# Both score halves of a head pair in one TensorE group, over two double banks of PSUM

## The chip, the core and the metric

The kernel runs on one core of a Trainium2 chip. The metric is the device time of one execution in microseconds. The core has a matrix engine (TensorE, PE in the profile; its weight loads are PEld), a vector engine (VectorE, DVE), an activation engine (ScalarE, ACT), GpSimd (POOL, which issues most loads here) and SyncE (SP, which issues the stores and the DMA transposes). Each takes its own instructions in the order written; semaphores hold them together. TensorE writes to PSUM, which has eight banks of 128 partitions x 512 fp32.

## The reference

Sparse causal attention over 8 batches, 8 heads, 576 positions and head size 64, and then an MLP with an ELU on its output rows.

```python
scores = scale * np.matmul(q, k.transpose(0, 1, 3, 2))
mask_local = (rel >= 0) & (rel < 32)                       # heads 0 to 3
mask_strided = (rel >= 0) & (pos[None, :] % 32 == pos[:, None] % 32)   # heads 4 to 7
attn = softmax of the masked scores
x = (attn @ v) as [4608, 512]
h = x @ w_in                                               # [512, 2048]
g = np.where(h > 0.0, h, np.exp(np.minimum(h, 0.0)) - 1.0)
out = g @ w_out                                            # [2048, 512], fp32
```

## The kernel before

The 4608 rows of x are cut into nine chunks of 512. The main loop runs over nb = 0 to 9; its iteration nb has 16 steps s, and each step issues, in this order: the attention pieces of gap 2s, `moe_in(nb, s)`, the pieces of gap 2s + 1, `moe_out(nb - 1, s)`. `moe_in` makes one [128 x 512] block of h: four products (L532) into a bank of the ring `hps`, the exponential on ACT (L553), a clamp on DVE (L560) and a maximum on DVE that also reads the bank (L562). `moe_out` adds four of the sixteen products of an output block (L572) in a bank of the ring `ops`; every fourth one is followed by the copy to SBUF on ACT (L576) and the store on SP. The schedule is manual: each engine's order is the order in which the program issues.

The attention of batch nb + 1 lies in the gaps of iteration nb. A batch has four pairs of heads: s0 and s1 (strided), l0 and l1 (local). Pair i takes its gaps from `start + pitch * i` on, by the offsets in `TIMES`: t_q and t_k (transposes of q and k on TensorE; left out for strided pairs from batch `BY_DMA` = 3 on and for local ones from batch `EARLY` = 4 on, where DMA transposes do it), two halves u = 0 and 1 of the scores, two halves of AV, x_out, and v_in. `scores(u)` makes four or six products of 64 rows each (L422) into a double bank, takes the exponential on ACT (L430) and multiplies with the mask on DVE (L437). `av(u)` multiplies the probabilities with v and a column of ones (L454) into one bank of `ring`, and DVE takes the reciprocal of the sums (L462) and scales (L463) into x. `x_out` transposes x on TensorE into a bank of `ring` (L490 strided, L503 local) and copies it to xT (ACT at L497 and L499 for strided pairs, DVE at L507 for local ones); from batch 4 on the pair l0 does this by a DMA transpose (L482). `halo` copies rows of v on DVE (L411), in the pair s1, two gaps ahead of its second AV. For batches 3 to 7 the list ends with

```python
(at[6] + (b > 1 and pr.strided), pr.x_out), (at[5] - 2, pr.halo)
```

so a strided pair's x_out comes one gap later than a local one's.

A `Ring` gives out its banks: one that was not used yet, or else the one used longest ago. `share` sets the four rings `sc` (scores), `hps`, `ops` and `ring` for each iteration. From the second iteration on `sc` has one double bank, `pair_a`; a second one, `pair_b`, serves the opening and is then split into the two banks `b_halves` for `hps`. `ops` has one bank, singles[3], wherever attention of batch 2 or later runs beside it.

Of the kernel before, what the change touches and what calls it, by code (L numbers as in the profile page):

```python
# [10 lines left out]
F32 = mybir.dt.float32  # L11
# [5 lines left out]
PSUM = bass.MemoryType.PSUM  # L17
# [13 lines left out]


PIECES = (-2, -1, 0, 2, 3, 5, 7, 0)
TIMES = (
    None,
    (4, 6, (-3, -2, 0, 2, 4, 6, 9, 3)),
    (6, 6, (-3, -2, 0, 2, 4, 6, 8, 0)),
    (2, 7, PIECES),
)


# [15 lines left out]
def kernel(  # L57
# [23 lines left out]
    inner = ctx.enter_context(ExitStack())  # L81
# [5 lines left out]

    ps = inner.enter_context(tc.tile_pool(name="ps", bufs=1, space=PSUM))
    pair_a = ps.tile([128, 2, 512], F32, tag="pair_a")
    singles = [ps.tile([128, 512], F32, tag=f"single{i}", name=f"single{i}")  # L90
               for i in range(4)]

    used = []

    class Ring:
        def __init__(self, *banks):
            self.banks = banks

        def next(self):

            for bank in self.banks:
                if all(bank is not u for u in used):
                    break
            else:
                bank = next(u for u in used if any(u is b for b in self.banks))
                used[:] = [u for u in used if u is not bank]
            used.append(bank)
            return bank


    rings = {}

    def share(sc, hps, ops, ring):
        rings.update(sc=Ring(*sc), hps=Ring(*hps), ops=Ring(*ops), ring=Ring(*ring))
# [2 lines left out]
    opening = ctx.enter_context(ExitStack())  # L117
    p_p0 = opening.enter_context(tc.tile_pool(name="probs0", bufs=8))
    p_k = opening.enter_context(tc.tile_pool(name="keys", bufs=1))
    ps_open = ctx.enter_context(ExitStack())  # L120
    ps_b = ps_open.enter_context(tc.tile_pool(name="ps_b", bufs=1, space=PSUM))
    pair_b = ps_b.tile([128, 2, 512], F32, tag="pair_b")

    def bf16_bank():
        return rings["ring"].next().bitcast(BF16)
# [32 lines left out]
    BY_DMA = 3  # L158
# [46 lines left out]
    def transpose_batch(b):  # L205

        if b >= BY_DMA:
            for name, to in (("q", qT), ("k", kT)):
                nc.sync.dma_start_transpose(out=to["str"][b % 2],
                                            in_=nat[name, "str"][b % 3])  # L210
        if b >= EARLY:
            for name, to, o in (("q", qT, 0), ("k", kT, 32)):
                for a in range(2):
                    nc.sync.dma_start_transpose(
                        out=to["loc"][b % 2][:, a, o:o + 640].rearrange(
                            "p (i r) -> p i r", r=128),
                        in_=nat[name, "loc"][b % 3][:, 640 * a:640 * a + 640])

    def load_batch(b):
        for name in "qkv":  # L220
            load_strided(b, name)
        for name in "qkv":
            load_local(b, name)
# [97 lines left out]
    class Pair:  # L321
# [89 lines left out]
                nc.vector.tensor_copy(t[0:32, :, 1:6, 0:D], t[96:128, :, 0:5, 0:D])  # L411

        def scores(self, u):
            sc = rings["sc"].next()
            blocks = self.blocks(u)
            for p, blk, bank, i, nk, nq in blocks:
                at, half = self.place(p, blk)
                d = slice(64 * half, 64 * half + 64)
                kind = "str" if self.strided else "loc"
                c = 0 if self.strided else LB * blk  # L420

                nc.tensor.matmul(sc[:, bank, i * nq:(i + 1) * nq],  # L422
                                 lhsT=kT[kind][self.b % 2][d, at, c:c + 128],
                                 rhs=qT[kind][self.b % 2][d, at, c:c + nq],
                                 start=True, stop=True)
            nk, nq = blocks[0][4:]
            w = len(blocks) // 2 * nq
            pr = (p_p if self.b else p_p0).tile([128, 648], BF16, tag="pr", name="pr")
            halves = pr[0:nk, 0:2 * w].rearrange("k (a x) -> k a x", a=2)
            nc.scalar.activation(halves, sc[0:nk, :, 0:w], ACT.Exp, scale=scale)  # L430
            if not self.strided:
                m = mask_l[:, 288 * u:288 * (u + 1)]
            elif u == 0:
                m = mask_s[0:126, 0:252]
            else:
                m = mask_s3[0:108, 0:324]
            nc.vector.tensor_tensor(halves, halves,  # L437
                                    m.unsqueeze(1).to_broadcast([nk, 2, w]),
                                    op=ALU.mult)
            self.pr[u] = pr  # L440
# [68 lines left out]
    def attention(b, start, pitch, at):  # L509


        gaps = {}
        pairs = [Pair(b, s, hp) for s in (True, False) for hp in range(2)]
        for i, pr in enumerate(pairs):
            for off, piece in ((at[0], pr.t_q), (at[1], pr.t_k),
                               (at[7], lambda pr=pr: pr.v_in(0)),
                               (at[7] + (b > 1), lambda pr=pr: pr.v_in(1)),
                               (at[2], lambda pr=pr: pr.scores(0)),
                               (at[3], lambda pr=pr: pr.scores(1)),
                               (at[4], lambda pr=pr: pr.av(0)),  # L520
                               (at[5], lambda pr=pr: pr.av(1)),
                               (at[6] + (b > 1 and pr.strided), pr.x_out), (at[5] - 2, pr.halo)):
                gaps.setdefault(start + pitch * i + off, []).append(piece)
        return gaps

# [10 lines left out]
    def moe_ahead(c, start, stop):  # L536

        for m in range(AHEAD):
            if start:
                ahead[m] = rings["hps"].next()  # L540
            moe_chunk(0, m, c, ahead[m], start, stop)
# [56 lines left out]
    def range_flag(row_ok16):  # L598
        cnt = rings["ring"].next()
        nc.tensor.matmul(cnt[0:1, 0:1], lhsT=row_ok16, rhs=ones, start=True, stop=True)  # L600
        nc.vector.tensor_scalar(flag, cnt[0:1, 0:1], scalar1=127.5, scalar2=None,
                                op0=ALU.is_le)

    def run(gaps, keys):
        for gap in sorted(g for g in gaps if g in keys):
            for piece in gaps[gap]:
                piece()
# [4 lines left out]
    for step in OPENING:  # L612
        pair, what = step.split(".")
        if pair == "moe":
            if step == parts[0]:

                ps_open.close()
                ps_h = inner.enter_context(tc.tile_pool(name="ps_h", bufs=1, space=PSUM))
                b_halves = [ps_h.tile([128, 512], F32, tag=f"half{i}", name=f"half{i}")
                            for i in range(2)]  # L620
                rings["hps"] = Ring(*b_halves, singles[3])
            moe_ahead(int(what), step == parts[0], step == parts[-1])
        else:
            pairs[pair].step(what)
# [13 lines left out]
    for nb in range(n_chunks + 1):  # L638

        if nb + 1 < B:  # L640
            gaps = attention(nb + 1, *TIMES[min(nb + 1, 3)])
            if nb == 0:
                share([pair_a], b_halves + singles[3:], [], singles[:3])
            elif nb + 1 < EARLY:
                share([pair_a], b_halves, singles[3:], singles[:3])
            else:
                share([pair_a], b_halves + singles[:1], singles[3:], singles[1:3])
        else:
            gaps = {}
            share([], b_halves + singles[:1], singles[2:], singles[1:2])  # L650
        if nb + 3 < B:
            load_batch(nb + 3)
        for s in range(MC):
            if s == 6 and nb > 0 and nb + 2 < B:
                transpose_batch(nb + 2)
            run(gaps, (2 * s,) if s else range(-10, 1))
            if nb < n_chunks:
                moe_in(nb, s)
            run(gaps, (2 * s + 1,))
            if nb == B and s == 4:  # L660
                range_flag(row_ok16)
            if nb > 0:
                moe_out(nb - 1, s)
        run(gaps, range(2 * MC, 1000))
        if nb + 1 == B:
            row_ok16 = range_check()
# [163 lines left out]
```

## Time and profile before

| what | value |
|---|---|
| runs | 334.74, 334.87, 336.98 us; median 334.87 |
| profiled execution | span 333.1 us from its first to its last instruction; the page gives no other time of it |
| TensorE | busy 310.6 us (93%) |
| DVE | busy 246.2 us (74%) |
| ACT | busy 177.8 us (53%) |
| POOL | busy 147.5 us (44%) |
| PE share of the chain that ended last | 81% |
| L572, 128x512 | 145.5 us busy, 379 ns mean |
| L532, 128x512 | 112.2 and 38.8 us busy (two kinds of bank), 383 and 381 ns mean |
| L430, exponential of scores | 39.0 us busy, 650 ns mean |
| L562, DVE maximum | 70.2 and 25.5 us busy, 688 ns mean |
| L576, output copy | 21.1 us busy, 587 ns mean |

A row of the order of time has a start, a duration, an engine, a line, an operation, out<-in by the program's names, the shapes and a count of instructions that follow one another; brackets at its end hold the idle time before it and what ended it. Products are pipelined, so one of them lasts longer than the step from its start to the next one's; the step is what PE's time is made of.

### The profile page before, as it was taken

What the parts mean: (1) busy time and instruction counts of PE and PEld (TensorE: products, weight loads), DVE (VectorE), ACT (ScalarE), POOL (GpSimd) and SP (SyncE); (2) the same over time, 40 slices, a digit from 0 to 9 for tenths busy, and PEclk for the clock granted to TensorE, in tenths of its full rate; (3) what the DMA queues carried; (4) which work ended last, traced back from release to release, by engine and by line L of the source; (5) the groups of instructions that cost most, each with busy time, mean ns of one, the idle gap of its engine ahead of it and who ended that gap; (6) DMA issues with size and microseconds to landing.
All of it is one profiled execution on the core that took longest, in us unless ns stands there. A gap on an engine that the chain in (4) does not pass through costs nothing.

```text
span 333.1 us, 6197 instructions
## 1 busy us (share of the span) xinstructions
PE 310.6 (93%) x2262; PEld 151.8 (46%) x2262; DVE 246.2 (74%) x540; ACT 177.8 (53%) x316; POOL 147.5 (44%) x233
## 2 busy tenths in 40 slices
PE   1886878999999999999999999999999999999993
PEld 0553444555544454444444444444444444444441
DVE  6686689786878778889788878887888666766500
ACT  3747967776446755554555455545554434444310
POOL 8977675998299699969796000000000000000000
PEclk9999979999999999999999999999999999999999
DMA  5999998999999999999999906310001010010111
GB/s 105 147 134 173 168 207 112 128 127 145 158 123 157 141 179 105 125 145 214 118 139 152 131 33 134 89 50 33 31 33 49 31 66 31 31 36 31 64 64 70
DMA packets 100091, 35.09 MB, mean 105 GB/s; under 512 B 77837, under 2 KB 95445, under 8 KB 100053
## 3 DMA queue, kind: packets, MB, share of 16 engines
q0 software_dynamic: 68016, 18.10, 56.4%
q1 hardware_dynamic: 32037, 16.52, 24.3%
q8 instruction: 19, 0.31, 0.5%
q14 instruction: 19, 0.16, 0.2%
HBM read 36.70 MB, written 9.44 MB: 139 GB/s over the span
## 4 chain that ended last, share of the span: by engine, by line
PE 81%; POOL 7%; DVE 4%; DMA 4%; issue 1%; ACT 1%; DVEq 0%; POOLq 0%; ACTq 0%
PE single L572 38%; PE half L532 25%; PE single L532 8%; PE pair_a L422 3%; PE single L454 3%; DMA v_loc<-in_v_dram 2%; DMA w_in_sb<-in_moe_w_in_dram 2%; POOL v_raw L173 1%; POOL v_loc L185 1%; POOL k_str L173 1%; DVE g_sb L562 1%; PE single L490 1%; PE single L366 1%; PE single L503 1%; DVE x_l L463 1%
## 5 line engine op out<-in xcount | busy, mean ns | idle before, releaser
L572 PE MATMUL single<-w_out_sb,g_sb 128*128 128x512 bf16 x576 | 145.5, 379 | 0.0
L532 PE MATMUL half<-xT,w_in_sb 128*128 128x512 bf16 x428 | 112.2, 383 | 0.5 <-DVE xT L507 0.5
L553 ACT ACTIVATE e_sb<-half 128x512 f32<-128x512 f32 x107 | 63.9, 598 | 75.9 <-PE half L532 70.4
L560 DVE TENSOR_SCALAR e_sb<-e_sb 128x512 bf16<-128x512 f32 x139 | 62.2, 447 | 47.1 <-ACT e_sb L553 44.7
L572 PEld LDWEIGHTS <-g_sb 128*128 128x128 bf16 x576 | 52.8, 98 | 59.0 <-issue 1.1
L532 PEld LDWEIGHTS <-w_in_sb 128*128 128x128 bf16 x576 | 51.0, 99 | 53.1 <-issue 1.0
L562 DVE TENSOR_TENSOR g_sb<-e_sb,half 128x512 bf16<-128x512 bf16 x102 | 70.2, 688 | 3.8
L430 ACT ACTIVATE pr<-pair_a 128x576 bf16<-128x576 f32 (+2 forms) x60 | 39.0, 650 | 10.6 <-PE pair_a L422 10.4
L532 PE MATMUL single<-xT,w_in_sb 128*128 128x512 bf16 x148 | 38.8, 381 | 0.0
L553 ACT ACTIVATE e_sb<-single 128x512 f32<-128x512 f32 x37 | 22.1, 598 | 26.8 <-PE single L532 23.6
L576 ACT COPY o_sb<-single 128x512 f32<-128x512 f32 x36 | 21.1, 587 | 20.0 <-PE single L572 19.7
L454 PEld LDWEIGHTS <-pr 128*128 128x128 bf16 (+3 forms) x352 | 21.6, 111 | 16.4 <-issue 3.4
L562 DVE TENSOR_TENSOR g_sb<-e_sb,single 128x512 bf16<-128x512 bf16 x37 | 25.5, 688 | 1.4
L185 POOL DMA_DIRECT2D v_loc<-in_v_dram x32 | 24.0, 779 | 3.2 <-DMA k_loc<-in_k_dram 1.4
L173 POOL DMA_DIRECT2D k_str<-in_k_dram x32 | 20.7, 692 | 5.8 <-DMA w_out_sb<-in_moe_w_out_dram 3.2
L173 POOL DMA_DIRECT2D v_raw<-in_v_dram x32 | 21.0, 718 | 3.1 <-DMA k_str<-in_k_dram 1.9
L173 POOL DMA_DIRECT2D q_str<-in_q_dram x28 | 17.8, 659 | 10.2 <-DMA k_loc<-in_k_dram 6.9
L463 DVE TENSOR_TENSOR x_l<-single,rden 96x384 bf16<-96x384 f32 x32 | 17.7, 553 | 1.1
L437 DVE TENSOR_TENSOR pr<-pr,mask_l 128x576 bf16<-128x576 bf16 x32 | 14.4, 453 | 3.1 <-ACT pr L430 2.9
L463 DVE TENSOR_TENSOR x_s<-single,rden 126x256 bf16<-126x256 f32 (+1 forms) x32 | 15.7, 491 | 1.1
L437 DVE TENSOR_TENSOR pr<-pr,mask_s 126x504 bf16<-126x504 bf16 (+1 forms) x32 | 14.3, 449 | 1.3 <-ACT pr L430 1.1
L454 PE MATMUL single<-v_loc,pr 128*128 128x65 bf16 x192 | 12.3, 204 | 0.9 <-DVE v_loc L411 0.7
(96 smaller groups left out, 246.1 us busy)
## 6 DMA issues: line engine op xcount, KB each, us to landing
out_dram<-o_sb SPq DMA_DIRECT2D x36, 256.0 KB, 2.4
v_loc<-in_v_dram POOLq DMA_DIRECT2D x32, 72.0 KB, 6.8
k_str<-in_k_dram POOLq DMA_DIRECT2D x32, 67.5 KB, 4.3
v_raw<-in_v_dram POOLq DMA_DIRECT2D x32, 67.5 KB, 5.0
w_in_sb<-in_moe_w_in_dram POOLq DMA_DIRECT2D x4, 512.0 KB, 7.7
w_out_sb<-in_moe_w_out_dram POOLq DMA_DIRECT2D x4, 512.0 KB, 12.9
q_str<-in_q_dram POOLq DMA_DIRECT2D x28, 67.5 KB, 5.2
q_loc<-in_q_dram POOLq DMA_DIRECT2D x4, 288.0 KB, 6.4
```

Source lines behind the costliest of these rows:

```text
L173: engine.dma_start(out=t[0:108, h].rearrange("p g d -> p (g d)"), in_=rows[h, :, 0:30, :].rearrange("t (r g) d -> t r (g d)", g=5))
L185: nc.gpsimd.dma_start(out=v_loc[b % 3][32:128, h, :, :D], in_=v[b, h].rearrange("(i p) d -> p i d", p=LB))
L430: nc.scalar.activation(halves, sc[0:nk, :, 0:w], ACT.Exp, scale=scale)
L437: nc.vector.tensor_tensor(halves, halves, m.unsqueeze(1).to_broadcast([nk, 2, w]), op=ALU.mult)
L454: nc.tensor.matmul(av[0:m, p, blk - b0, :], lhsT=self.pr[u][0:nk, o:o + m], rhs=vt[0:nk, 2 * self.hp + p, blk, :], start=True, stop=True)
L463: nc.vector.tensor_tensor(self.x[0:nq, b0:b0 + n].rearrange("q g p d -> q p g d"), av[0:nq, :, 0:n, 0:D], r.unsqueeze(3).to_broadcast([nq, ...
L532: nc.tensor.matmul(hps, lhsT=w_in_sb[:, c, m * 128:(m + 1) * 128], rhs=xT[:, c, nb * N_TILE:(nb + 1) * N_TILE], start=start, stop=stop)
L553: nc.scalar.activation(e_sb, hps, ACT.Exp)
L560: nc.vector.tensor_scalar(e1_sb, e_sb, scalar1=1.0, scalar2=1.0, op0=ALU.min, op1=ALU.subtract)
L562: nc.vector.tensor_tensor(g_of[nb][:, m, :], e1_sb, hps, op=ALU.max)
L572: nc.tensor.matmul(ops, lhsT=g_of[nb][:, m, kk * 128:(kk + 1) * 128], rhs=w_out_sb[:, m, :], start=(m == 0), stop=(m == MC - 1))
L576: nc.scalar.copy(o_sb, ops)
```

## The change

For batches 3 to 7 the offsets `PIECES` = (-2, -1, 0, 2, 3, 5, 7, 0) give way to `WHOLE`: both score halves at 0, AV at 3 and 4, x_out at 6 for every pair. The half u = 0 always goes to `pair_a`, u = 1 always to `pair_b`. `pair_b` is now allocated once, and `b_halves` are views of its two banks. From the iteration with batch 3 on these halves are in the ring for AV and for x_out, and `hps` takes single banks: two with batch 3, as before, and three later, as before. Whenever `pair_b` is given out as a whole, both halves count as just used. The halo moves with the second AV, to offset 2.

```diff
+WHOLE = (-2, -1, 0, 0, 3, 4, 6, 0)
 TIMES = (
...
-    (2, 7, PIECES),
+    (2, 7, WHOLE),
 )
...
+    pair_b = ps.tile([128, 2, 512], F32, tag="pair_b")
+    b_halves = [pair_b[:, i, :] for i in range(2)]
...
-        def next(self):
-
-            for bank in self.banks:
+        def next(self, of=None):
+
+            banks = self.banks if of is None else self.banks[of:of + 1]
+            for bank in banks:
                 if all(bank is not u for u in used):
                     break
             else:
-                bank = next(u for u in used if any(u is b for b in self.banks))
+                bank = next(u for u in used if any(u is b for b in banks))
                 used[:] = [u for u in used if u is not bank]
             used.append(bank)
+            if bank is pair_b:
+                used[:] = [u for u in used if all(u is not h for h in b_halves)]
+                used.extend(b_halves)
             return bank
...
         def scores(self, u):
-            sc = rings["sc"].next()
+            sc = rings["sc"].next(u if self.b >= BY_DMA else None)
...
-                               (at[6] + (b > 1 and pr.strided), pr.x_out), (at[5] - 2, pr.halo)):
+                               (at[6] + (b == 2 and pr.strided), pr.x_out), (at[5] - 2, pr.halo)):
...
             if nb == 0:
                 share([pair_a], b_halves + singles[3:], [], singles[:3])
+            elif nb + 1 < BY_DMA:
+                share([pair_a], b_halves, singles[3:], singles[:3])
             elif nb + 1 < EARLY:
-                share([pair_a], b_halves, singles[3:], singles[:3])
+                share([pair_a, pair_b], singles[1:3], singles[3:], b_halves + singles[:1])
             else:
-                share([pair_a], b_halves + singles[:1], singles[3:], singles[1:3])
+                share([pair_a, pair_b], singles[:3], singles[3:], b_halves)
         else:
             gaps = {}
-            share([], b_halves + singles[:1], singles[2:], singles[1:2])
+            share([], singles[:3], [singles[3], b_halves[0]], b_halves[1:])
```

More of the change, by code (lines that the diff above doesn't have):

```diff
@@ L119 @@
     p_k = opening.enter_context(tc.tile_pool(name="keys", bufs=1))
-    ps_open = ctx.enter_context(ExitStack())
-    ps_b = ps_open.enter_context(tc.tile_pool(name="ps_b", bufs=1, space=PSUM))
-    pair_b = ps_b.tile([128, 2, 512], F32, tag="pair_b")
     def bf16_bank():
@@ L615 @@
             if step == parts[0]:
[L617 to L620, printed above, removed]
                 rings["hps"] = Ring(*b_halves, singles[3])
```

## The prediction

> **What bounds the kernel now.** I read the page, then PE's waits, then the order of time in the five iterations whose attention is that of batches 3 to 7.
>
> ```profile
> span 333.1 us, 6197 instructions
> PE   1886878999999999999999999999999999999993
> PE half L532 <- DVE xT L507: 0.5, 1, 0.5
> ```
> The span is 333.1 us, and the median of the runs is 334.87, so 1.8 us lie around the span; I add differences to the median. The third line is the whole list of PE's waits from 88 us to 275 us: one wait of 0.5 us. In these stages TensorE runs back to back, and only what lengthens or shortens its own queue counts. DVE is the next engine: busy 27.13 of the 32.64 us from 226.59 to 259.23. The work between the products is therefore free as long as it is in time, and late as soon as its due time moves forward.
>
> The price of a group on PE is the step from its first start to the next group's:
>
> ```profile
> 160.28 1.03 PE L532 MATMUL half<-xT,w_in_sb 128*128 128x512 bf16 x4
> 161.14 1.03 PE L572 MATMUL single<-w_out_sb,g_sb 128*128 128x512 bf16 x4
> 162.10 0.28 PE L422 MATMUL pair_a<-qT_str,kT_str 64*128 64x126 bf16 x4
> 162.31 1.04 PE L532 MATMUL half<-xT,w_in_sb 128*128 128x512 bf16 x4
> 163.19 1.03 PE L572 MATMUL single<-w_out_sb,g_sb 128*128 128x512 bf16 x4
> 164.15 0.32 PE L422 MATMUL pair_a<-qT_str,kT_str 64*128 64x108 bf16 x6
> 164.40 1.04 PE L532 MATMUL single<-xT,w_in_sb 128*128 128x512 bf16 x4
> ```
> Four full products take 0.86 us (160.28 to 161.14), 0.216 each. Ahead of scores the step is 0.96: entry into the 64-row form costs **0.10**. The four scores start within 0.065 us, in two couples (a couple runs side by side on the two halves of the rows), and the last couple needs 126/512 of 0.216 = 0.05; yet the next product starts 0.145 after it. So leaving costs **0.09**.
>
> **Gain: two groups become one.** Four pairs in each of five batches lose one entry and one exit: 20 x 0.19 = **3.8 us**. The ten or twelve products themselves remain, and no other work covers this; it comes straight off PE. Bounds: 2.0 if only the entry is saved, 4.2 if the slower first product after the scores (0.226 for 0.216) goes too.
>
> The Trainium skill (TensorEngine Tiling (Array Packing), Key Properties) says that changing the tiling mode, and not just the tile, drains TensorE. A full drain would be the product's 379 ns less its 216 ns step, an estimate of 0.16 us for each switch; 40 switches would then give 6.5 us in place of 3.8, and the sum below would end at 338.6. The trace shows smaller switches, so I keep 3.8.
>
> **Cost: x_out comes sooner than DVE.** Between the second AV product (L454) and the pair's transposes (L490, L503) DVE must do the reciprocal (L462) and the multiplication (L463). Before, a strided pair has three gaps for it (offsets 5 to 8), a local one two (5 to 7). After, all have two (4 to 6), and AV changes parity. An AV in an even gap stands before moe_in, so DVE takes its work ahead of that step's activation; one in an odd gap stands behind moe_in, and its DVE work queues behind the whole chain L553, L560, L562:
>
> ```profile
> 181.02 1.03 PE L532 MATMUL half<-xT,w_in_sb 128*128 128x512 bf16 x4
> 181.89 0.36 PE L454 MATMUL single<-v_loc,pr 128*128 128x65 bf16 x6
> 182.09 0.60 ACT L553 ACTIVATE e_sb<-half 128x512 f32<-128x512 f32 x1 [1.33 <-PE half L532]
> 182.72 0.43 DVE L560 TENSOR_SCALAR e_sb<-e_sb 128x512 bf16<-128x512 f32 x1
> 183.18 0.69 DVE L562 TENSOR_TENSOR g_sb<-e_sb,half 128x512 bf16<-128x512 bf16 x1
> 183.78 0.18 DVE L462 RECIPROCAL rden<-single 96x6 f32<-96x6 f32 x1
> 184.00 0.55 DVE L463 TENSOR_TENSOR x_l<-single,rden 96x384 bf16<-96x384 f32 x1
> ```
> From AV to normalised x it is 184.55 - 181.89 = 2.66 us in an odd gap; ACT had stood idle 1.33, so it is a chain and no backlog. In an even gap (189.01 to 190.81) it is 1.80. Due time after two gaps: AV 0.20 + two groups 1.73 + the transposes of the first half (0.10 strided, 0.13 local), which need only the first AV: 2.04 to 2.06. That a transpose runs up to the second half and then waits shows at 158.13: six transposes took 0.58 in place of 0.42, x being ready at 158.35; a release takes 0.06.
>
> Pair by pair, for batches 4 to 7 (starts 2, 9, 16, 23):
> - s0: AV in gaps 5 and 6, x_out in 8. The second AV is even, but its 0.7 us of DVE work now stand right behind the first AV's, which end 2.56 after an odd gap. 2.56 + 0.70 - 1.02 (the second AV's later start) = 2.24; + 0.06 - 2.04 = **0.25** (0.19 to 0.30 by how far DVE's records overlap).
> - s1: gaps 12 and 13, x_out 15: odd. 2.68 + 0.06 - 2.04 = 0.70. The halo copy (0.49, now in gap 11) and the first normalisation stand ahead and push this step's L560 back by about 0.2; I take **0.80** (0.66 to 0.95).
> - l0: x_out is a DMA from SP's queue; PE waits for nothing. It is issued earlier, behind nothing new.
> - l1: gaps 26 and 27, x_out 29: odd. 2.66 + 0.06 - 2.06 = **0.66** (0.60 to 0.75).
>
> **Cost: two exponentials ahead of an output copy.** There is one bank for L572 (singles[3]), freed by the copy L576 of every fourth moe_out, and in gap 23 the scores of l1 stand just before such a moe_out:
>
> ```profile
> 183.91 0.30 PE L422 MATMUL pair_a<-qT_loc,kT_loc 64*128 64x96 bf16 x6
> 184.01 0.60 ACT L553 ACTIVATE e_sb<-single 128x512 f32<-128x512 f32 x1 [1.33 <-PE single L532]
> 184.51 0.65 ACT L430 ACTIVATE pr<-pair_a 128x576 bf16<-128x576 f32 x1
> 185.22 0.59 ACT L576 COPY o_sb<-single 128x512 f32<-128x512 f32 x1
> 186.21 1.04 PE L572 MATMUL single<-w_out_sb,g_sb 128*128 128x512 bf16 x4
> ```
> The copy ends at 185.81 and its bank is wanted at 186.21. With both exponentials ahead, counted from the scores: L553 0.10, exponentials 0.60 and 1.15 to 1.25, copy 1.70 to 2.00, its end 2.29 to 2.59, release 2.35 to 2.65. PE wants the bank after scores 0.35 and two groups 1.73, at 2.08, since the second score group no longer lies between. That is 0.27 to 0.57; I take **0.40**. Queued behind the waiting L572 is all of PE.
>
> The Trainium skill (TensorEngine Tiling (Array Packing), PSUM Bottleneck) warns that tiling speeds up TensorE but not the emptying of PSUM. By the trace this bites only here: ACT is busy 17.87 of 32.64 us, so as an engine it does not become the bound.
>
> **Edits at nothing.** The scores' second half needs pair_b, the ring of AV and x_out since the last pair. After s0 the ACT copies of x_out (0.61 + 0.20, behind L576) free it at about the same 0.1 us at which it is wanted, since x_out has itself waited; without that wait it would cost 0.2 instead. Masks come earlier and hide under the three gaps to AV. hps keeps its two or three banks; the last iterations only rename theirs.
>
> **Batch 3** transposes its local q and k on PE: t_q (0.48 with its entry) lies in s1's two gaps and leaves 0.3 of its wait, and t_k now stands behind x_out's copies on ACT, so that l0's scores wait some 0.2 for kT. l0's x_out, on PE here, has t_q of l1 ahead of it and is in time. With s0 0.25, l1 0.66 and the copy 0.40: 1.8 us.
>
> **Sum.** Batches 4 to 7: 0.25 + 0.80 + 0.66 + 0.40 = 2.11 each, 8.4; batch 3 1.8; less 3.8: **+6.4 us, 341.3**. All low ends with the full gain give 4 x 1.72 + 1.2 - 4.2 = +3.9; all high ends with a gain of 2.0 give 4 x 2.57 + 2.4 - 2.0 = +10.7.
>
> **Rivals.**
> - *Faster: DVE is early.* The masks leave DVE before AV instead of between the two AVs; were x ready within 2.04 of the odd AV, x_out would wait nowhere. Where the copy's wait then remains, 5 x 0.4 - 3.8 = -1.8 gives 333.1; where the freer engines hide that too, 331.1. It decides from a latency 0.64 shorter. Against it: ACT's idle 1.33 above; the odd latency is a chain that no mask is part of. Chance 0.08: 0.05 for 331.1, 0.03 for 333.1.
> - *A draw.* Half of each wait, with the whole gain: 0.5 x 10.2 - 3.8 = +1.3, 336.2. Waits are not independent: where PE has waited, DVE and ACT have caught up. For it: s0's wait spares the ring's. Chance 0.13.
> - *The halves of pair_b count as one buffer.* Then the second AV waits for the first's normalisation: 2.6 or 1.8 against 1.02, some 1.6 + 0.8 + 1.6 + 0.8 a batch, 24 us, less part of the x_out waits: about 355. Against it: x's halves were told apart at 158.13. Chance 0.04.
> - The forecast, waits as laid out: 0.75.
>
> **Numbers.** About 1% (3.3 us) can be told from no change. Faster by more 0.05; within 1% 0.16 (the draw, and 333.1); slower by more 0.79 (the forecast and the one buffer). The forecast's own range is 338.8 to 345.6; for 8 in 10 I reach down into the draw: 336.5 to 345.6.
>
> **What would show it.** Right: L422 in 20 groups of ten or twelve with one entry each; in PE's waits L490 on DVE x_s some 5 us, L503 on x_l some 3.3, L572 on ACT's L576 some 2; an iteration of batch 5 near 33.9 us in place of 32.64. Wrong: no PE wait on L463, an AV-to-x latency under 2.0 in gaps 13 and 27, or a step before and after the scores that does not shrink.

## The result and the profile after

The changed kernel takes 374.08 us (median of 4 runs), the one before in the same comparison 334.81: a ratio of 1.120, 95% interval 1.115 to 1.125. The forecast was 341.3 in a range of 336.5 to 345.6. The sign was right, the size was off by a factor of six.

The page of the changed kernel. The busy row of PE has lost its nines from the second fifth on, and comes back to them only at the end.

```profile
span 372.2 us, 6161 instructions
PE   1785877787797989888988898889888999979994
```

Between 88 and 275 us TensorE had one wait of 0.5 us before. Now the list of PE's waits over the whole run (columns: total, times, longest) holds these; lines of the changed file stand four lines lower (L458 is AV, L536 moe_in, L576 moe_out, L566 the maximum, L467 the normalisation):

```profile
PE pair_b L536 <- DVE g_sb L566: 10.4, 15, 1.0
PE pair_b L458 <- DVE x_s L467: 10.3, 8, 1.4
...
PE pair_b L458 <- DVE x_l L467: 8.6, 8, 1.8
...
PE pair_b L576 <- DVE flag L605: 1.8, 1, 1.8
```

All of them write to pair_b, and each waits for DVE. A stretch of the order of time in the pair s1 shows what for:

```profile
196.30 0.32 PE L458 MATMUL pair_b<-v_str,pr 126*128 126x65 bf16 x4
...
197.51 0.61 DVE L415 COPY v_loc<-v_loc 32x1280 bf16<-32x1280 bf16 x1
...
198.04 0.16 DVE L466 RECIPROCAL rden<-pair_b 126x4 f32<-126x4 f32 x1
198.24 0.42 DVE L467 TENSOR_TENSOR x_s<-pair_b,rden 126x256 bf16<-126x256 f32 x1
...
198.71 0.37 PE L458 MATMUL pair_b<-v_str,pr 108*128 108x65 bf16 x6 [1.23 <-DVE x_s L467]
```

The first AV (196.30) writes half 0, the second (198.71) half 1. The second starts 0.05 us after DVE has finished reading half 0. It needs nothing from there: its own bank had been free since the exponential of the scores. In the built program the first product of each of the sixteen second AVs of batches 4 to 7 waits by a semaphore for exactly that multiplication, which reads the other half (8 and 8 waits in the list above), so the wait was put there when the program was made; the chip only obeys it. The same is in `moe_in` of the early iterations, where `hps` is made of the two views and each block waits for the maximum of the block before, and at the very end, where the range flag's bank and one of `ops` are the two halves:

```profile
65.82 0.69 DVE L566 TENSOR_TENSOR g_sb<-e_sb,pair_b 128x512 bf16<-128x512 bf16 x1
...
66.56 1.02 PE L536 MATMUL pair_b<-xT,w_in_sb 128*128 128x512 bf16 x3 [0.84 <-DVE g_sb L566]
...
331.02 0.16 PE L604 MATMUL pair_b<-ones,row_ok 128*1 128x1 bf16 x1
333.01 1.02 PE L576 MATMUL pair_b<-w_out_sb,g_sb 128*128 128x512 bf16 x3 [1.83 <-DVE flag L605]
```

Where the time went, by iteration. An iteration is counted from the first weight load of a chunk's moe_in to the next chunk's (chunk 8: to the first load of the moe_out behind it); all 576 of these loads are in each trace. us:

| iteration (attention of batch) | before | after | difference |
|---|---|---|---|
| to the start of chunk 1 | 55.75 | 56.77 | +1.0 |
| chunk 1 (batch 2) | 36.17 | 47.43 | +11.3 |
| chunk 2 (batch 3) | 35.34 | 40.60 | +5.3 |
| chunk 3 (batch 4) | 32.81 | 37.69 | +4.9 |
| chunks 4, 5, 6 (batches 5 to 7) | 32.64 each | 37.68, 37.57, 37.57 | +14.9 |
| chunk 7 | 27.63 | 27.63 | 0 |
| chunk 8 | 27.83 | 29.71 | +1.9 |

Together that is, but for rounding, the difference of the spans, 39.1 us. Chunk 1 is worst, although its offsets were not changed at all: PE waits 10.1 us there for the maximum. Not all of chunk 2's 5.3 is the change: in this execution the granted clock stood at half from 122.5 to 125.9 us (in the one before at 45.4 to 48.8, ahead of chunk 1), which can be up to 1.7 us of it.

One thing went as planned: the two score groups are one.

```profile
183.57 1.03 PE L576 MATMUL single<-w_out_sb,g_sb 128*128 128x512 bf16 x4
...
184.53 0.28 PE L426 MATMUL pair_a<-qT_str,kT_str 64*128 64x126 bf16 x4
184.65 0.31 PE L426 MATMUL pair_b<-qT_str,kT_str 64*128 64x108 bf16 x6
...
184.89 1.04 PE L536 MATMUL single<-xT,w_in_sb 128*128 128x512 bf16 x4
```

From the product group at 183.57 to the next at 184.89 it takes 1.32; less that group's own 0.864, 0.46 for ten score products. Before it was (0.96 - 0.864) + 0.21 and (0.96 - 0.864) + 0.25 in two groups, together 0.65. The gain is 0.19 per pair, the forecast's figure; the step of the first product behind a scores group is 0.01 longer than of the others (0.226 for 0.216), which also happens once in place of twice; with it, and unrounded, a pair gains 0.21.

### The profile page after: what moved, and what is told of

It is laid out like the page before. It is cut to its first block, busy times and chain, and to the rows that moved or that the text cites. A ratio compares the mean times of both kernels' runs of the same rounds, so it can differ in the third digit from the quotient of the medians.

```text
span 372.2 us, 6161 instructions
## 1 busy us (share of the span) xinstructions
PE 308.9 (83%) x2222; PEld 154.6 (42%) x2262; DVE 245.7 (66%) x540; ACT 174.6 (47%) x316; POOL 146.6 (39%) x233
## 4 chain that ended last, share of the span: by engine, by line
PE 60%; DVE 15%; ACT 10%; issue 5%; POOL 4%; DMA 3%; SPq 1%; ACTq 0%; DVEq 0%; POOLq 0%
PE single L536 22%; PE single L576 19%; ACT e_sb L557 6%; PE pair_b L536 6%; PE pair_b L576 6%; DVE g_sb L566 5%; DVE e_sb L564 4%; DVE x_l L467 2%; DMA q_stage<-in_q_dram 2%; PE pair_b L458 2%; DVE x_s L467 1%; ACT pr L434 1%; DMA v_raw<-in_v_dram 1%; PE pair_a L426 1%; PE pair_b L426 1%
## 5 line engine op out<-in xcount | busy, mean ns | idle before, releaser
L557 ACT ACTIVATE e_sb<-single 128x512 f32<-128x512 f32 x118 | 70.6, 598 | 126.2 <-PE single L536 120.8
L536 PE MATMUL single<-xT,w_in_sb 128*128 128x512 bf16 x459 | 120.1, 380 | 1.7 <-issue 0.8
L576 PE MATMUL single<-w_out_sb,g_sb 128*128 128x512 bf16 x463 | 119.5, 381 | 2.0 <-issue 1.4
L566 DVE TENSOR_TENSOR g_sb<-e_sb,single 128x512 bf16<-128x512 bf16 x117 | 80.5, 688 | 4.4
L536 PEld LDWEIGHTS <-w_in_sb 128*128 128x128 bf16 x576 | 53.2, 98 | 69.4 <-issue 15.0
L576 PEld LDWEIGHTS <-g_sb 128*128 128x128 bf16 x576 | 53.5, 98 | 62.4 <-issue 4.9
L536 PE MATMUL pair_b<-xT,w_in_sb 128*128 128x512 bf16 x96 | 27.0, 383 | 14.3 <-DVE g_sb L566 10.4
L458 PEld LDWEIGHTS <-pr 128*128 128x128 bf16 (+3 forms) x352 | 21.4, 109 | 37.3 <-issue 26.5
L434 ACT ACTIVATE pr<-pair_a 128x576 bf16<-128x576 f32 (+2 forms) x40 | 25.5, 636 | 7.4 <-PE pair_a L426 7.3
L557 ACT ACTIVATE e_sb<-pair_b 128x512 f32<-128x512 f32 x26 | 15.6, 599 | 23.9 <-PE pair_b L536 23.1
L576 PE MATMUL pair_b<-w_out_sb,g_sb 128*128 128x512 bf16 x94 | 23.5, 379 | 2.0 <-DVE flag L605 1.8
L580 ACT COPY o_sb<-single 128x512 f32<-128x512 f32 x30 | 17.7, 590 | 11.3 <-PE single L576 11.3
L434 ACT ACTIVATE pr<-pair_b 128x576 bf16<-128x576 f32 (+2 forms) x24 | 16.3, 677 | 1.3 <-PE pair_b L426 1.3
L566 DVE TENSOR_TENSOR g_sb<-e_sb,pair_b 128x512 bf16<-128x512 bf16 x22 | 15.1, 688 | 0.8
L458 PE MATMUL pair_b<-v_str,pr 108*128 108x65 bf16 (+2 forms) x92 | 6.2, 197 | 10.3 <-DVE x_s L467 10.3
L441 DVE TENSOR_TENSOR pr<-pr,mask_s 126x504 bf16<-126x504 bf16 (+1 forms) x32 | 13.8, 457 | 1.3 <-ACT pr L434 1.2
```

Source lines behind the costliest of these rows:

```text
L441: nc.vector.tensor_tensor(halves, halves, m.unsqueeze(1).to_broadcast([nk, 2, w]), op=ALU.mult)
L458: nc.tensor.matmul(av[0:m, p, blk - b0, :], lhsT=self.pr[u][0:nk, o:o + m], rhs=vt[0:nk, 2 * self.hp + p, blk, :], start=True, stop=True)
L536: nc.tensor.matmul(hps, lhsT=w_in_sb[:, c, m * 128:(m + 1) * 128], rhs=xT[:, c, nb * N_TILE:(nb + 1) * N_TILE], start=start, stop=stop)
L557: nc.scalar.activation(e_sb, hps, ACT.Exp)
L566: nc.vector.tensor_tensor(g_of[nb][:, m, :], e1_sb, hps, op=ALU.max)
L576: nc.tensor.matmul(ops, lhsT=g_of[nb][:, m, kk * 128:(kk + 1) * 128], rhs=w_out_sb[:, m, :], start=(m == 0), stop=(m == MC - 1))
```

## Experiments

Two theories. A: the two views of one PSUM tile are held as one buffer, so every write into one half waits for the readers of the other. B: the new order itself (AV and x_out too early for DVE) costs the time. Totals of one kernel spread by a few us with the clock that was granted (the first experiment ran 344.0 and 343.6 at a mean of 0.987, 341.4 and 339.9 at 0.999), so what matters by less is read from the iterations.

### Two buffers, the whole new schedule

```diff
-    pair_b = ps.tile([128, 2, 512], F32, tag="pair_b")
-    b_halves = [pair_b[:, i, :] for i in range(2)]
...
+                b_halves = [ps_h.tile([128, 512], F32, tag=f"half{i}", name=f"half{i}")
+                            for i in range(2)]
...
-            sc = rings["sc"].next(u if self.b >= BY_DMA else None)
+            two = self.b >= BY_DMA and u == 1
+            if two:
...
+                sc = [b_halves[0], b_halves[1]]
...
-            nc.scalar.activation(halves, sc[0:nk, :, 0:w], ACT.Exp, scale=scale)
+            if two:
+                for a in range(2):
+                    nc.scalar.activation(halves[:, a, :], sc[a][0:nk, 0:w], ACT.Exp,
+                                         scale=scale)
```

> The changed kernel with its whole schedule (both score halves in one group, AV at 3 and 4, x_out at 6), but the two banks are two buffers again: the opening has its own double bank, the main loop two single banks half0 and half1; the second score half goes into these two, with one exponential for each in place of one over both. Theory A (the two views of pair_b are held as one buffer, so that a writer of one half waits for the readers of the other): nearly all of the 39 us comes back, and what stays is the forecast's sum, 338.8 to 345.6 us; the waits of L458's AV for the other half's normalisation are gone, and the x_out waits of 0.2 to 0.9 us appear. Theory B (the schedule itself costs it: AV and x_out come too early for DVE, whatever the buffers): stays above 365 us.

342.5 us, ratio 1.020 (1.011 to 1.028): A. Nothing of the order was touched, and 32 of the 39 us are gone; that the split exponential gives nothing of it back shows in the kernel with the old offsets below. Chunk 1 takes 36.17 again, chunk 8 27.83. PE's waits from 91 to 258 us are now led by the ones that the forecast had laid out (L504 and L517 are the transposes in this file, L477 the normalisation, L590 the output copy):

```profile
PE half L504 <- DVE x_s L477: 3.9, 6, 0.9
PE half L517 <- DVE x_l L477: 2.1, 4, 0.6
...
PE single L586 <- ACT o_sb L590: 0.2, 1, 0.2
```

and in s1 one sees the transposes of the first half, then the wait for the multiplication of the second:

```profile
213.80 0.28 PE L504 MATMUL half<-identity,x_s 126*128 126x126 bf16 x2
...
214.28 0.56 DVE L477 TENSOR_TENSOR x_s<-half,rden 108x384 bf16<-108x384 f32 x1
...
214.90 0.32 PE L504 MATMUL half<-identity,x_s 108*128 108x108 bf16 x3 [0.82 <-DVE x_s L477]
```

The output copy's wait stands where it was expected, in l1. It hardly shows in the list, which counts only the idle time behind a product's end: below, the product group ahead of the waiting one (224.16 to 225.19) ends 0.11 us before 225.30, but the step from its start is 1.143 in place of 0.863. The two exponentials of the second half take 0.72 together, for 0.65 of the one over both banks:

```profile
224.05 0.72 ACT L441 ACTIVATE pr<-half 128x288 bf16<-128x288 f32 x2
...
224.63 0.62 ACT L590 COPY o_sb<-single 128x512 f32<-128x512 f32 x1
...
225.30 1.02 PE L586 MATMUL single<-w_out_sb,g_sb 128*128 128x512 bf16 x4
```

### The old schedule on views

```diff
+    pair_b = ps.tile([128, 2, 512], F32, tag="pair_b")
+    b_halves = [pair_b[:, i, :] for i in range(2)]
...
-                b_halves = [ps_h.tile([128, 512], F32, tag=f"half{i}", name=f"half{i}")
-                            for i in range(2)]
```

> The kernel before with its whole schedule, and only the allocation of the changed one: pair_b stays allocated, and half0 and half1, here banks of hps, are views of it. Theory A: PE waits in moe_in for the maximum (L562) of the block before: some 11 us more in the iteration of chunk 1 and about as much in that of chunk 2 (two banks, both views), 4 to 5 us in each of those of chunks 3 to 6 (two views and one single bank), little at the ends: 360 to 378 us in all. Theory B: as before, 335 us.

398.32 us, ratio 1.188 (1.179 to 1.197). The allocation alone, without any change of order, costs more than the change itself, because here the views serve `hps`, the ring of every moe_in, to the end. Chunk 1 takes 13.8 us more (in this execution with 3.4 us at half the clock, up to 1.7 of it), chunk 2 12.0, chunks 3 to 6 4.6 to 5.4 each, near what A gives; chunks 7 and 8 take 6.4 and 7.2 more and what lies ahead of chunk 1 4.5, which I had left out, so the total is above the 378 that I gave. One line has most of it:

```profile
PE pair_b L531 <- DVE g_sb L561: 53.9, 62, 2.4
```

### Two buffers, the old offsets

```diff
-WHOLE = (-2, -1, 0, 0, 3, 4, 6, 0)
+WHOLE = (-2, -1, 0, 2, 3, 5, 7, 0)
```
(and the extra gap for a strided pair's x_out again)

> As the one with two buffers again, but with the old offsets from the fourth batch on (score halves at 0 and 2, AV at 3 and 5, x_out at 7 or 8): the new places of the banks and the two exponentials for the second half, without merged groups. Theory A: 334 to 336 us, as before: places and exponentials cost nothing, and the gain of 3.8 us is not there. Theory B: as before too. Should it be slower by more than 2 us, the split exponential costs, and the other two kernels have to be read against this one.

335.51 us, ratio 1.002 (0.998 to 1.006). The new places of the banks and the split exponential cost little: chunks 3 to 6 take 32.89 us in place of 32.64 to 32.81, 0.1 to 0.25 each. So nearly all of the differences between the other two-buffer kernels and the one before come from order and grouping.

### Two buffers, AV one gap earlier

```diff
-WHOLE = (-2, -1, 0, 0, 3, 4, 6, 0)
+WHOLE = (-2, -1, 0, 0, 2, 3, 6, 0)
```

> As the one with two buffers again, but AV at offsets 2 and 3 in place of 3 and 4, so that three gaps lie between the second AV and x_out. Theory A with the forecast's laid-out x_out waits: these (0.25 + 0.80 + 0.66 us a batch) go, and the copy's wait of 0.4 us or less and perhaps some wait of the first AV for its mask stay: 331.5 to 336 us, 5 to 8 us below the one with AV at 3 and 4. If the x_out waits are not what costs there, the two are equal. Theory B: above 365 us.

337.69 us, ratio 1.010 (1.005 to 1.014); chunks 4 to 6 fall from 33.97 to 32.85. The x_out waits are gone, as expected, but the total is above the range that I gave. A wait took their place that I had not listed: the second AV of s0 needs the second half of v_in, which DVE reaches only behind moe_in's work.

```profile
PE half L468 <- DVE v_str L407: 2.1, 5, 0.8
```

### The same with v copied two gaps earlier

```diff
-WHOLE = (-2, -1, 0, 0, 2, 3, 6, 0)
+WHOLE = (-2, -1, 0, 0, 2, 3, 6, -2)
```

> Two buffers, AV at offsets 2 and 3, x_out at 6 as in the run with AV at 2 and 3; new is that both halves of the copy of v (v_in, L407) come two gaps earlier, at -2 and -1. There the second AV of s0 waited 0.4 to 0.5 us for the second half of that copy in each of five batches. If merged groups are worth 0.19 us each and only waits hid it: the wait for v_str goes and an iteration of batches 5 to 7 falls from 32.85 to 32.4 us (before: 32.64), the time by some 2 us to about 335.5. If merging gains nothing: the wait moves to another place and the iteration stays at 32.8.

333.71 us, ratio 0.998 (0.995 to 1.001). Chunks 4 to 6 take 32.36 us, as expected, and the wait for v_str is gone. Of the 0.8 us that merging gives a batch, 0.3 are left over; small waits hold the rest: in chunk 5, 0.1 us each at the scores of s1 and l0, and 0.12 and 0.21 ahead of the first AVs of s1 and l1.

### Two buffers, x_out late, three banks in the ring

```diff
-WHOLE = (-2, -1, 0, 0, 3, 4, 6, 0)
+WHOLE = (-2, -1, 0, 0, 3, 4, 7, 0)
...
-                               (at[6] + (b == 2 and pr.strided), pr.x_out), (at[5] - 2, pr.halo)):
+                               (at[6] + (b > 1 and pr.strided), pr.x_out), (at[5] - 2, pr.halo)):
...
-                share([pair_a], singles[:3], singles[3:], b_halves)
+                share([pair_a], singles[1:3], singles[3:], b_halves + singles[:1])
```

> Two buffers, both score halves at 0, AV at 3 and 4 as in the changed kernel, but x_out late again (7 local, 8 strided, as before the change), which asks for a third bank in the ring (half0, half1, singles[0]), so hps has two banks. Forecast's terms: the x_out waits (measured 0.22, 0.99 and 0.68 us a batch with two buffers) go, the wait of L586 for the output copy (0.28) stays, the gain of 0.8 a batch stays: an iteration of batches 5 to 7 takes 32.1 us in place of 33.97, and the kernel 332 us, some 2.5 below the one before. Rival: two banks of hps are too few beside two exponentials in a row; then moe_in waits for L562's kind of maximum and the iteration is 32.6 or more.

Chunks 4 to 6 take 32.07 to 32.15 us where 32.1 was expected: the x_out waits are gone and two banks of hps are enough. The total, 336.16 (ratio 1.004, 1.000 to 1.007), missed the 332: batch 3, which I had not looked at, takes 36.40 in place of 35.34. One scores group there waits for a local pair's x_out that was given its bank a moment before:

```profile
PE half L431 <- DVE xT L521: 1.8, 1, 1.8
```

That is less than half of the miss. Of the rest, the clock is a likely part, but no run isolates it: none of this kernel's twelve executions had a mean granted clock above 0.992, while 15 of the 29 of the kernel before had 0.995 or more.

### Every pair one gap later

```diff
-    (2, 7, WHOLE),
+    (3, 7, WHOLE),
...
+                               (at[6] + (2 if b > 2 else b > 1) * pr.strided, pr.x_out), (at[5] - 2, pr.halo)):
```
(offsets -2, -1, 0, 0, 3, 4, 6, 0; three ring banks)

> As the one with late x_out and three ring banks, but every pair starts one gap later (3, 10, 17, 24), with x_out at 8 (strided) and 6 (local) from there, so that the scores of l1 no longer stand between moe_in and a moe_out that ends in an output copy. The output copy's wait of 0.28 a batch goes: an iteration of batches 5 to 7 takes 31.85 us, the kernel 331 us, 3.8 below the one before. If that wait is not from the two exponentials ahead of the copy, it stays at 32.1.

333.67 us, ratio 0.995 (0.992 to 0.998): half a per cent below the kernel before, less than I gave. The copy's wait is gone from PE's list; but l1's x_out waits: its transposes take 0.628 us in chunk 5 in place of 0.257, so chunks 4 to 6 take 32.17 and not 31.85. Its two AVs stand in gaps 27 and 28, as those of s0 in the forecast do: the second one's DVE work comes right behind the first one's. I had worked that out for s0 and did not apply it here.

```profile
PE half L517 <- DVE x_l L477: 1.0, 5, 0.2
```

### x_out late, with batch 3 and l1 mended

```diff
-                               (at[6] + (b > 1 and pr.strided), pr.x_out), (at[5] - 2, pr.halo)):
-                gaps.setdefault(start + pitch * i + off, []).append(piece)
+                               (at[6] + (b > 1 and pr.strided) - (b == 3 and not pr.strided), pr.x_out), (at[5] - 2, pr.halo)):
+                gaps.setdefault(start + pitch * i - (b > 3 and i == 3) + off, []).append(piece)
```

> The run with late x_out and three ring banks, with two places mended: batch 3 issues a local pair's x_out at 6 in place of 7, so that the scores' half bank isn't the one that this x_out was just given (there PE waited 1.8 us once), and in batches 4 to 7 the pair l1 starts one gap sooner (22 in place of 23), so that its exponentials stand further ahead of the output copy. If the copy's wait of 0.28 us comes from the two exponentials ahead of it, an iteration of batches 5 to 7 takes 31.8 us in place of 32.07 and that of batch 3 34.6 in place of 36.4; the kernel 331 us, 3.5 to 4 below the one before. If that wait only moves to another place, 32.1 stays and the kernel is at 332.5.

332.57 us, ratio 0.9935 (0.9902 to 0.9968), the lowest median of all; its interval overlaps those of the two others that came out below the kernel before (v copied earlier, every pair one gap later), so they cannot be ranked. Both halves of what I expected were missed in part. Chunk 5 takes 32.04 us, not 31.8: the copy's wait is gone from its steps, but the scores of l1 take 0.605 in place of 0.361, since, one gap sooner, their half bank is still being read by l0's normalisation. In chunk 6 this wait is longer, and the iteration takes 32.32:

```profile
246.94 0.20 PE L431 MATMUL half<-qT_loc,kT_loc 64*128 64x96 bf16 x1
247.46 0.28 PE L431 MATMUL half<-qT_loc,kT_loc 64*128 64x96 bf16 x5 [0.32 <-DVE x_l L477]
```

The iteration of batch 3 takes 35.53, not 34.6: with x_out back at 6, l1's transposes there wait for their normalisation again (1.01 us, 0.31 before), and the output copy's wait is there too (a step of 1.21 in place of 0.86).

## Why the prediction was wrong, and where it was right

**The step that failed** is the wait between the two halves of pair_b, for which the sum has no term: under edits at nothing, the banks were priced as if each half were a buffer of its own. That they count as one buffer was named as a rival, and it got a chance of 0.04. The evidence against it was that the two parts of x were told apart at 158.13. That was a tile in SBUF, and a reader that waits for its writer; I carried it over to a PSUM tile and to a writer that waits for a reader, of which the trace of before shows no case: there the halves were two tiles of their own. Which of the two differences counts, no run here shows. The two kernels with one allocation changed settle it: the old order on views costs 63 us, the new order on two tiles 7.

**The rival's price was half of the bill.** It put 4.8 us a batch on the second AV and ended at about 355, 20 of the 39 us. In chunk 5 of the changed kernel the group ahead of it takes 2.43, 2.15, 2.59 and 1.51 us in place of 0.86: waits of 1.56, 1.28, 1.72 and 0.65, together 5.2, near that price. But I priced only the ring of AV, also in batch 3, where a third bank of the ring keeps the second AV from waiting (the 16 waits are all in batches 4 to 7). The views serve `hps` in the iterations before the new offsets begin (11.3 us in chunk 1), the transposes of q and k in chunk 2 (PE waits of 1.8 and 1.2 us), and `ops` beside the flag in chunk 8 (1.9 us). The change's text had them in view, and I had filed them under edits at nothing: "the last iterations only rename theirs".

**The rest of the sum holds once the buffers are two.** Per batch, forecast against the steps of chunk 5 in the first experiment:

| term | forecast | measured |
|---|---|---|
| x_out of s0 | 0.25 | 0.478 - 0.257 = 0.22 |
| x_out of s1 | 0.80 (0.66 to 0.95) | 1.253 - 0.257 = 1.00 |
| x_out of l1 | 0.66 | 0.938 - 0.257 = 0.68 |
| output copy | 0.40 (0.27 to 0.57) | 1.143 - 0.863 = 0.28 |
| merged groups, four pairs | -0.76 | -0.84 (0.21 a pair) |
| iteration | +1.35 | 33.97 - 32.64 = +1.33 |

Over the five iterations with the new offsets it is +6.9 us against +6.4; that of batch 3 takes 1.56 more, where the sum gives 1.8 - 0.76 = 1.04. The s1 wait was longer than its range because the halo copy and the first normalisation ran right ahead: DVE started L477 at 214.28, 2.42 us after AV. In the changed kernel itself these waits hardly show (PE's list there has 0.2 to 0.6 us for the transposes): the second AV had waited for DVE already, and DVE caught up meanwhile. Two costs that add up on paper hid each other, but the larger one is what the forecast lacked.

**The draw and the early DVE** were both wrong: no wait was halved (the copy's came nearest, 0.28 for 0.40), and the odd-gap chain is what it was: with two buffers l1's normalised x comes 2.67 us after its AV, before 2.66.

**The switch of the tiling mode** cost 0.10 and 0.09 us, as the rows of before had it. The Trainium skill (TensorEngine Tiling (Array Packing), Key Properties) has a drain there, and the trace agrees that a switch costs time. The full 0.16 us a switch that I had estimated for it did not come out.

## What to carry to other kernels

Two views of one tile are not two buffers until the waits of the built program, or a trace, say so; for every ring that a change builds from views, ask which wait the second view would get, and price it in every stage that uses the ring, also those whose order is not touched. To tell an aliasing cost from a schedule's cost, change the allocation alone and the schedule alone. And when a group moves earlier, look for all that its consumer needs (v, a bank, a mask), since the next wait is usually one more operand that was in time only by accident.

## What was not expected of the hardware

Nothing in the chip was at fault: the waits are in the program. What stood out is how exactly the short score products follow from rows of before: entry 0.10, exit 0.09, and couples on the two row halves side by side. Ten strided score products in one group took 0.36 us to the next group's start in every kernel where nothing held them up.
